# Attention with gated experts: the products with V of a pair in four groups instead of nine, and a batch's gating over more steps

## The chip, the cores and the metric

The kernel runs on one core of one Trainium2 chip. The metric is the device time of one execution in microseconds (us), the median over runs.

## The reference

Attention over 8 batches of 8 heads, 576 rows, head width 64, in which scores more than tau below their row's maximum are dropped; its output is the input of a mixture of 8 experts, of which each row takes the best two.

```python
scores = scale * np.matmul(q, k.transpose(0, 1, 3, 2))
thresh = np.max(scores, axis=-1, keepdims=True) - tau
scores = np.where(scores >= thresh, scores, -1000000000.0)
attn = np.exp(scores - np.max(scores, axis=-1, keepdims=True))
attn = attn / (np.sum(attn, axis=-1, keepdims=True) + 1e-09)
x = np.matmul(attn, v)                       # rows: 8 * 576, columns: 8 heads * 64
noisy = x @ w_gate + np.log1p(np.exp(x @ w_noise)) * noise
top2 = ...                                   # the two largest of 8, softmax over the two
out[mask] += weight * (np.maximum(x[mask] @ w1[e], 0.0) @ w2[e])     # per expert e
```

## The kernel before

Two heads of a batch are a **pair**; there are 32 pairs, four to a batch. The 2 x 576 score rows of a pair are cut into 9 tiles of 128 rows: tile j = 0 holds the last 64 rows of both heads, tiles 1 to 8 the first 512 rows of the two heads in turn. One tile is one **step**. Pair n begins at step g = 9n, and everything else that belongs to it is placed at a step counted from g, by the table `SCHED` and the loop at the end of `attention`. Steps of successive pairs overlap: what pair n does in its step 12 stands in step 3 of pair n + 1. Below, **place** p (0 to 8) is the step modulo 9, so the places of a pair's own tiles.

Within a step the phases run in the order (0, 1, 2, 3, 4, 5, 8, 6, 7), and each engine executes its own instructions in exactly that order:

- phase 0: `oev` (L387), ScalarE copies a finished half of the products with V out of PSUM into `ot`.
- phase 1: `scores` (L247), TensorE, one step ahead of the rest: tile j + 1 goes into one of two double banks `sp`. Each of two column halves takes two matmuls (L271), tile 0 three.
- phase 2: `rowmax`: VectorE scales the scores and takes the row maximum (L282), ScalarE takes exp (L284). Phase 3: `mask` (L307), VectorE, two steps behind. Phase 4: `threshold` (L292), ScalarE.
- phase 5: the products with V, the gating, the norm of the rows and `xlpart`/`xev`.
- phase 8: loads and `split_q`, `split_k`: ScalarE makes the high part of the next pair's q and k (L186, L198), GpSimd the low part, SyncE's queue spreads them (L220). k is at place 0 and q at place 2.
- phase 6: `ptile` (L310), three steps behind: TensorE transposes the masked tile in four parts (L319) into a PSUM bank and ScalarE copies it out (L322; L324 and L325 for tile 0). Phase 7: `pcorner` (L340 to L342) and `prem` (L333, L334), the same for the columns left over.

**The products with V.** `avpiece(n, i, kt)` (L385) multiplies one of five row blocks kt of V with one of two column pieces i of the transposed tiles (320 and 256 columns). Each call is a matmul for either head, in 64 of the array's columns each, and the hardware runs each as two: the profile shows four. The fifth block, `ptr`, uses 64 rows as well. `SCHED["av"]` gives the step of each call, `oev` the step of the copy. `xlpart` (L404, L405) then transposes the two halves of `ot` back and multiplies them with the gate's weights, at the steps `xl`; its first half has two blocks of 128, its second half two of 128 and one of 64.

**PSUM banks.** Four banks `tp0` to `tp3` serve all of these: `bank` takes the one that was released longest ago, when the program is written, and `done` gives it back. A product with V holds its bank from the first block to its `oev`; the others take and release theirs in one step.

**Gating.** At the end of a batch nine stages (L514 to L622) turn the gate's logits into slots; they go between GpSimd, VectorE, ScalarE and TensorE. Ten `gate_put` calls (L627, L628) on GpSimd's queue then write the table of slots. Before, stage i stands at step x + i + (i > 3), x being the step behind the second `xl`, and the first put at x + 11. The last two batches' puts and the last batch's stages have steps of their own (`START`, `LAST`), which the change leaves alone. The experts' first work is counted from step G = 288; their first read of the table, `tokens` (L837, SyncE's queue), stands at G - 35 = 253.

Of the kernel before, what the change touches and what calls it, by code (L numbers as in the profile page):

```python
# [43 lines left out]
WARM = 10  # L44

SCHED = dict(
    lag=2, mlag=2, lead=1, corner=8, rem=11, norm=11, av=((10, 11, 12, 13, 14), (15, 17, 17, 18, 19)), oev=(15, 20),
    xl=(16, 22), q=2, k=0, oevp=0, pieces=((0, 320), (320, 576)), order=(0, 1, 2, 3, 4, 5, 8, 6, 7),
    rec=12, xs=4, qsc="act", qs=0)


LAST = dict(
    av=((11, 11, 12, 12, 12), (12, 12, 12, 12, 12)), oev=(13, 13), xl=(14, 14), rec=13, norm=12)
# [7 lines left out]
    gate=(6, 7, 7, 8, 9, 9, 10, 11, 11), put=(12, 12, 12, 13, 13, 13, 13, 13, 13, 13), tokb=13, ixb=17,  # L61
# [4 lines left out]
@with_exitstack  # L66
def tile_attention_moe(ctx: ExitStack, tc, q, k, v, tau, wgn, noise, noise_r, w1, w2, out, x_dram, table, stage):
    nc = tc.nc
    const = ctx.enter_context(tc.tile_pool(name="const", bufs=1))
    cap = CAP  # L70
    nover = -(-max(N - cap, 0) // 128)
    slots = cap + 128 * nover
    state = dict(cap=cap, nover=nover, slots=slots)
    with tc.manual_schedule(), ExitStack() as c:
        work = c.enter_context(tc.tile_pool(name="work", bufs=1))
        psum = c.enter_context(tc.tile_pool(name="psum", bufs=1, space=PSUM))
        experts = Experts(tc, const, work, psum, state, w1, w2, out, x_dram, table, stage)
        attention(tc, const, work, psum, state, q, k, v, tau, wgn, noise, noise_r, out, x_dram, table, experts)
        experts.run(lambda: overflow_count(tc, const, work, state) if nover else None)
    if nover:  # L80
        with ExitStack() as c:
            overflow(c, tc, const, state, w1, w2, out, x_dram, table)
# [23 lines left out]
def early_batches():  # L106

    return max(B - 2, 0)
# [22 lines left out]
def attention(tc, const, work, psum, state, q, k, v, tau, wgn, noise, noise_r, out, x_dram, table, experts):  # L131
# [91 lines left out]
    xl = work.tile([128, HP, 32], F32, name="xl", tag="xl")  # L223
# [142 lines left out]
    ot, av = {}, {}  # L366
# [270 lines left out]
    def at(g, phase, f, *a):  # L637
        ev.setdefault((g, phase), []).append((f, a))
# [9 lines left out]
    lag = SCHED["lag"] + MLAG - 1  # L648
    G = 9 * NP
# [5 lines left out]
    for n in range(NP):  # L655
        g = 9 * n
        for j in range(9):
            at(g + j - d["lead"], 1, scores, n, j)
            at(g + j, 2, rowmax, n, j)
            at(g + j + MLAG, 3, mask, n, j)  # L660
            at(g + j, 4, threshold, n, j)
            at(g + j + lag, 6, ptile, n, j)
        at(g + d["corner"], 7, pcorner, n)
        at(g + d["rem"], 7, prem, n)
        at(g + d["norm"], 5, norm, n)
        at(g + d["rec"], 5, invert, n)
        if n == NP - 1:
            d = dict(SCHED, **LAST)
        for i in range(len(PIECES)):
            for kt in range(5):  # L670
                at(g + d["av"][i][kt], 5, avpiece, n, i, kt)
            at(g + d["oev"][i], d["oevp"], oev, n, i)
        for i in range(2):
            at(g + d["xl"][i], 5, xlpart, n, i)
            at(g + d["xl"][i], 5, xev, n, i)
        if n + 2 < NP:
            at(g if n else 9, 2, load, n + 2)
        if n + 1 < NP:
            at(g + d["qs"], 8, scale_q, n + 1)
            at(g + d["q"], 8, split_q, n + 1)  # L680
            at(g + d["q"], 8, spread, n + 1, "qs", [nc.sync])
            at(g + d["k"], 8, split_k, n + 1)
            at(g + d["k"], 8, spread, n + 1, "ks", [nc.sync])
        for f in parts[cut[n]:cut[n + 1]]:
            at(g + 6, 8, f)
        if n % HP == HP - 1:
            b = n // HP
            x = d["xl"][1] + 1
            for i in range(NB):
                at(g + x + (0 if b >= early_batches() else SCHED["xs"] + 2 * i), 5, xstore, b, i)  # L690
            late = experts and n == NP - 1
            if b == early_batches():
                at(g + x, 5, bump)
            for i, f in enumerate((gate_sum, gate_abs, gate_exp, gate_soft, gate_max, gate_hot, gate_rank,
                                   gate_slot, gate_slot2)):
                at(G + START["gate"][i] if late else g + x + i + (i > 3), 5, f, b)
            for i in range(2 * NB):
                to = g + x + 11 + i
                if experts and b >= B - 2:
                    to = G + START["put" if late else "put0"][i]  # L700
                at(to, 5, gate_put, b, i // 2, i % 2)
# [516 lines left out]
```

## Time and profile before

| | us |
|---|---|
| median of 3 runs | 1482.6 |
| lowest and highest run | 1479.03, 1483.6 |
| profiled execution | 1472.27 |
| its span, first to last instruction | 1470.5 |
| granted TensorE clock, mean | 0.993 |

The attention's 32 pairs take the first 606 us or so, the experts the rest; from about 525 us on the experts' first reads of the table, gathers and weights stand between the attention's instructions. The profile gives busy time by engine, an ordered list of instructions with their start (the timeline), and the waits. A bracket at the end of a timeline row is the idle time of that engine ahead of the instruction and what ended it; a row without one started without a wait. Matmuls overlap, so their durations add up to more than the time they take: what counts is from one start to the next. "128\*64" behind an operation is the part of the array used, rows by columns.

### The profile page before, as it was taken

What the parts mean: (1) busy time and instruction counts of PE and PEld (TensorE: products, weight loads), DVE (VectorE), ACT (ScalarE), POOL (GpSimd) and SP (SyncE); (2) the same over time, 40 slices, a digit from 0 to 9 for tenths busy, and PEclk for the clock granted to TensorE, in tenths of its full rate; (3) what the DMA queues carried; (4) which work ended last, traced back from release to release, by engine and by line L of the source; (5) the groups of instructions that cost most, each with busy time, mean ns of one, the idle gap of its engine ahead of it and who ended that gap; (6) DMA issues with size and microseconds to landing.
All of it is one profiled execution on the core that took longest, in us unless ns stands there. A gap on an engine that the chain in (4) does not pass through costs nothing. (4 is left out here: it accounts for less than half of the span.)

```text
span 1470.5 us, 26196 instructions
## 1 busy us (share of the span) xinstructions
PE 1435.7 (98%) x8750; PEld 1187.0 (81%) x8750; DVE 886.9 (60%) x2477; ACT 702.3 (48%) x1447; POOL 661.1 (45%) x1040
## 2 busy tenths in 40 slices
PE   8999999999999999997999999999999999999995
PEld 6777676767677776786998999999999989989884
DVE  7888888888888888644554344454454543543410
ACT  7888888888888887421222122132232221221210
POOL 4337575757575766454152262252342522521612
PEclk9999999999999999999999999999999999999998
DMA  7768686868686757356666376386375474573422
GB/s 198 188 164 214 164 223 161 218 168 223 161 217 165 193 154 194 83 123 149 172 150 152 86 164 147 87 186 157 81 186 142 115 171 120 133 170 89 69 29 31
DMA packets 189512, 220.48 MB, mean 150 GB/s; under 512 B 64453, under 2 KB 112541, under 8 KB 188353
## 3 DMA queue, kind: packets, MB, share of 16 engines
q1 hardware_dynamic: 162176, 178.91, 44.6%
q0 software_dynamic: 27200, 39.88, 16.3%
q8 instruction: 71, 1.16, 0.3%
q14 instruction: 65, 0.52, 0.1%
HBM read 103.25 MB, written 60.61 MB: 111 GB/s over the span
## 5 line engine op out<-in xcount | busy, mean ns | idle before, releaser
L284 ACT ACTIVATE e<-ns,nm 128x576 f32<-128x576 f32 x288 | 223.2, 775 | 37.1 <-DVE ns L282 34.4
L307 DVE SCALAR_TENSOR_TENSOR p<-ns,thr,e 128x576 f32<-128x576 f32 x256 | 222.3, 869 | 21.6 <-ACT thr L292 20.8
L282 DVE TENSOR_SCALAR_CACHE_REDUCE ns<-sp 128x576 f32<-128x576 f32 x288 | 214.4, 744 | 22.1 <-PE sp L271 17.7
L319 PEld LDWEIGHTS tp<-ident,p 128*128 128x128 f32 x1024 | 110.3, 143 | 99.7 <-ACT ot L391 23.1
L322 ACT ACTIVATE pt<-tp 128x512 f32<-128x512 f32 x256 | 150.9, 590 | 54.3 <-PE tp L319 53.5
L385 PE MATMUL tp<-pt,vt 128*64 128x256 f32 (+1 forms) x1024 | 176.5, 429 | 0.0
L319 PE MATMUL tp<-ident,p 128*128 128x128 f32 x1024 | 167.6, 286 | 0.0
L271 PE MATMUL sp<-ks,qh 128*128 128x288 f32 x496 | 159.6, 335 | 2.9 <-DVE ns L282 2.9
L963 POOL DMA_INDIRECT out<-m_y,ix x54 | 87.7, 1623 | 151.5 <-DVE m_y L1001 138.7
L963 POOL DMA_INDIRECT out<-m_y,sx x43 | 67.7, 1574 | 194.7 <-DVE m_y L944 160.3
L271 PE MATMUL sp<-ks,ql 128*128 128x288 f32 x496 | 138.3, 296 | 0.2 <-DMA ql<-loq 0.2
L923 ACT ACTIVATE m_p<-m_tp 128x384 fp32r<-128x384 f32 (+1 forms) x66 | 32.6, 494 | 211.1 <-PE m_tp L921 211.0
L944 DVE TENSOR_SCALAR m_y<-m_sp,gw 128x512 f32<-128x512 f32 (+1 forms) x43 | 32.3, 751 | 152.8 <-PE m_sp L942 144.2
L199 POOL TENSOR_TENSOR lok<-kr,hik 128x640 fp32r<-128x640 f32 x31 | 57.3, 1849 | 139.7 <-ACT hik L198 139.3
L871 POOL DMA_INDIRECT m_p<-x_rows,sx x71 | 70.1, 987 | 83.2 <-DMA stage<-m_p 45.5
L271 PEld LDWEIGHTS sp<-ks,qh 128*128 128x128 f32 x496 | 93.7, 189 | 5.0 <-DVE ns L282 3.2
L628 POOL DMA_INDIRECT slot_table<-pay,sl x80 | 87.8, 1097 | 17.5 <-issue 10.8
L271 PEld LDWEIGHTS sp<-ks,ql 128*128 128x128 f32 x496 | 94.2, 190 | 0.4 <-issue 0.4
L923 ACT ACTIVATE m_qh<-m_tp 128x384 fp32r<-128x384 f32 (+1 forms) x11 | 5.6, 506 | 181.8 <-PE m_tp L921 181.8
L385 PEld LDWEIGHTS tp<-pt,vt 128*64 128x64 f32 x1024 | 57.0, 136 | 42.6 <-issue 26.2
L921 PE MATMUL m_tp<-m_pt,m_pt 128*128 128x384 f32 (+1 forms) x396 | 72.6, 340 | 0.0
L921 PE MATMUL m_tp<-m_vt,m_pt 128*128 128x384 f32 (+1 forms) x264 | 71.7, 346 | 0.0
(386 smaller groups left out, 3503.2 us busy)
## 6 DMA issues: line engine op xcount, KB each, us to landing
m_qr<-w SPq DMA_DIRECT2D x85, 256.0 KB
qh<-hiq SPq DMA_DIRECT2D x124, 144.0 KB
ql<-loq SPq DMA_DIRECT2D x124, 144.0 KB
stage<-m_p SPq DMA_DIRECT2D x63, 256.0 KB
m_kr<-w SPq DMA_DIRECT2D x43, 256.0 KB
kr<-k SPq DMA_DIRECT2D x32, 320.0 KB
out<-zeros SPq DMA_DIRECT2D x19, 512.0 KB
qr<-q SPq DMA_DIRECT2D x32, 288.0 KB
```

The costliest lines, as they stand in the source:

```text
L199: nc.gpsimd.tensor_tensor(lo, x, hi.bitcast(F32), op=ALU.subtract)
L271: nc.tensor.matmul(o, q_, k_, start=(i == 0), stop=(i == len(parts) - 1))
L282: nc.vector.tensor_scalar(ns, sp[:, :, 0:HALF], -1.0 / math.sqrt(D), None, op0=ALU.mult, op1=ALU.min, accum_out=nm)
L284: nc.scalar.activation(e, ns, AF.Exp, bias=nm, scale=-1.0)
L307: nc.vector.scalar_tensor_tensor(p, ns, thr, e, op0=ALU.is_le, op1=ALU.mult, accum_out=ssum[n][:, c:c + 1])
L319: nc.tensor.transpose(tp[:, kt, :], p[:, 128 * kt:128 * kt + 128], ident)
L322: nc.scalar.activation(pt[n][:, s, :, c0:c0 + 128], tp, AF.Copy)
L385: nc.tensor.matmul(o[64 * s:64 * s + 64, 0:c1 - c0], w, x, start=(kt == 0), stop=(kt == 4))
L628: st = nc.gpsimd.indirect_dma_start(out=table, out_offset=bass.IndirectOffsetOnAxis(ap=d["sl"][0:m, i, c:c + 1], axis=0), in_=d["pay"][0:m ...
L871: self.nc.gpsimd.indirect_dma_start(out=r[0:m], out_offset=None, in_=x, in_offset=bass.IndirectOffsetOnAxis(ap=self.tok[e][2][0:m, t:t + 1 ...
L921: nc.tensor.matmul(ps[:, 0:n], w[:, 128 * c:128 * c + 128], x[:, c, 0:n], start=(i == 0), stop=(i == len(ops) - 1))
L963: st = self.nc.gpsimd.indirect_dma_start(out=out, out_offset=bass.IndirectOffsetOnAxis(ap=idx, axis=0), in_=y, in_offset=None, compute_op= ...
```

## The change

Two tables and the two lines that read them are edited. Products with V: piece 0 goes from steps 10, 11, 12, 13, 14 to 11, 11, 13, 13, 13, piece 1 from 15, 17, 17, 18, 19 to 15, 15, 17, 17, 17. The copies go from 15 and 20 to 14 and 18, the second `xl` from 22 to 21; the first stays at 16. By place, the products stood at 1 (two pairs' at once), 2, 3, 4, 5, 6, 8 and 0 and stand at 2, 4, 6 and 8 now; the copy of piece 1 goes from place 2 to place 0 and the second `xl` from place 4 to place 3. The gating's stages, counted from the pair's g, go from 23, 24, 25, 26, 28, 29, 30, 31, 32 to 22, 24, 25, 26, 28, 29, 32, 33, 35, the first of the ten puts from 34 to 37.

```diff
 SCHED = dict(
-    lag=2, mlag=2, lead=1, corner=8, rem=11, norm=11, av=((10, 11, 12, 13, 14), (15, 17, 17, 18, 19)), oev=(15, 20),
-    xl=(16, 22), q=2, k=0, oevp=0, pieces=((0, 320), (320, 576)), order=(0, 1, 2, 3, 4, 5, 8, 6, 7),
-    rec=12, xs=4, qsc="act", qs=0)
+    lag=2, mlag=2, lead=1, corner=8, rem=11, norm=11, av=((11, 11, 13, 13, 13), (15, 15, 17, 17, 17)), oev=(14, 18),
+    xl=(16, 21), q=2, k=0, oevp=0, pieces=((0, 320), (320, 576)), order=(0, 1, 2, 3, 4, 5, 8, 6, 7),
+    rec=12, gate=(0, 2, 3, 4, 6, 7, 10, 11, 13), put=15, xs=4, qsc="act", qs=0)
...
-                at(G + START["gate"][i] if late else g + x + i + (i > 3), 5, f, b)
+                at(G + START["gate"][i] if late else g + x + SCHED["gate"][i], 5, f, b)
             for i in range(2 * NB):
-                to = g + x + 11 + i
+                to = g + x + SCHED["put"] + i
```

TensorE, before, at places 2 to 4 of one pair. `tp2_3471` is bank tp2, its tile numbered 3471; `p` and `pr` are masked tiles (`pr` is tile 0), and the words in brackets name the engines whose semaphores the instruction waits on.

```order
L319 MATMUL tp1_3465<-ident_100,p_135 128x128 [waits DVE_49,Activation_49]
...
L333 MATMUL tp2_3471<-ident_100,p_135 128x128 [waits Activation_49]
...
L385 MATMUL tp0_3423<-pt1_3235,vt0_1687 64x320 x2
L319 MATMUL tp3_3500<-ident_100,pr0_3443 128x128 [waits DVE_49,Activation_49]
...
L404 MATMUL tp1_3518<-ident_100,ot0_3296 128x2x64 [waits Activation_49]
...
L385 MATMUL tp0_3423<-pt1_3235,vt0_1687 64x320 x2
L319 MATMUL tp2_3529<-ident_100,p_135 128x128 [waits DVE_49,Activation_49]
```

The same places of the same pair in the changed kernel:

```order
L319 MATMUL tp2_3465<-ident_100,p_135 128x128 [waits DVE_49,Activation_49]
...
L333 MATMUL tp3_3471<-ident_100,p_135 128x128 [waits Activation_49]
...
L404 MATMUL tp0_3489<-ident_100,ot0_3270 128x2x64 [waits Activation_49]
...
L319 MATMUL tp2_3507<-ident_100,pr0_3440 128x128 [waits DVE_49,Activation_49]
...
L385 MATMUL tp1_3444<-pt1_3236,vt0_1693 64x320 x4
L385 MATMUL tp1_3444<-ptr1_3237,vt0_1693 64x320 [waits Activation_49]
L385 MATMUL tp1_3444<-ptr1_3237,vt0_1693 64x320
L319 MATMUL tp3_3531<-ident_100,p_135 128x128 [waits DVE_49,Activation_49]
```

The products with V (L385) have left place 3, and `xlpart` (L404) has come into it, ahead of the transposes of tile 0. In the changed kernel those go into tp2, the bank of tile 8's transposes one place earlier. Before, they had tp3, and the next user of tile 8's bank was `xlpart` at place 4.

ScalarE, before, from exp of tile 0 at place 0 (the first row) to the copy of tile 8 at place 2 (the last but one):

```order
L284 ACTIVATE e0_3383<-ns0_3379,nm0_3380 128x576 [waits DVE_49,Activation_49]
L292 ACTIVATE thr0_3381<-nm0_3380,atau_120 128x1
L186 ACTIVATE qr1_3115<-qr1_3115,scale_118 128x576 [waits DMAHW0_49]
L198 ACTIVATE hik0_3395<-kr1_3114 128x640 [waits DMAHW2_49,DMAHW3_49,DMAHW1_49,Pool_49]
L322 ACTIVATE pt1_3235<-tp1_3403 128x4x128 [waits PE_49]
L284 ACTIVATE e1_3418<-ns1_3414,nm1_3415 128x576 [waits DVE_49,Activation_49]
L322 ACTIVATE pt1_3235<-tp2_3426 128x4x128 [waits PE_49]
L391 ACTIVATE ot0_3296<-tp3_3311 128x256
L284 ACTIVATE e2_3440<-ns2_3438,nm1_3415 128x576 [waits DVE_49,Activation_49]
...
L198 ACTIVATE hiq0_3449<-qr1_3115 128x576 [waits DMAHW1_49,DMAHW6_49,DMAHW0_49,DMAHW7_49,Activation_49,Pool_49]
L322 ACTIVATE pt1_3235<-tp1_3465 128x4x128 [waits PE_49]
L334 ACTIVATE ptr1_3236<-tp2_3471 128x512 [waits PE_49]
```

And the same stretch in the changed kernel:

```order
L391 ACTIVATE ot0_3270<-tp2_3305 128x256
L284 ACTIVATE e0_3384<-ns0_3380,nm0_3381 128x576 [waits DVE_49,Activation_49]
L292 ACTIVATE thr0_3382<-nm0_3381,atau_120 128x1
L186 ACTIVATE qr1_3116<-qr1_3116,scale_118 128x576 [waits DMAHW0_49]
L198 ACTIVATE hik0_3396<-kr1_3115 128x640 [waits DMAHW2_49,DMAHW3_49,DMAHW1_49,Pool_49]
L322 ACTIVATE pt1_3236<-tp3_3404 128x4x128 [waits PE_49]
L284 ACTIVATE e1_3419<-ns1_3415,nm1_3416 128x576 [waits DVE_49,Activation_49]
L322 ACTIVATE pt1_3236<-tp0_3424 128x4x128 [waits PE_49]
L284 ACTIVATE e2_3437<-ns2_3435,nm1_3416 128x576 [waits DVE_49,Activation_49]
...
L198 ACTIVATE hiq0_3449<-qr1_3116 128x576 [waits DMAHW1_49,DMAHW6_49,DMAHW0_49,DMAHW7_49,Activation_49,Pool_49]
L322 ACTIVATE pt1_3236<-tp2_3465 128x4x128 [waits PE_49]
L334 ACTIVATE ptr1_3237<-tp3_3471 128x512 [waits PE_49]
```

The copy of piece 1 (L391) has moved from between the copies of places 1 and 2 to the head of the stretch. What stands between tile 5's copy at place 8 and tile 8's copy at place 2 is the same set of instructions in both kernels (the two corner copies, L341 and L342, stand just ahead of both pieces).

## The prediction

> **What bounds the kernel now.** I read the page first, then the stages, TensorE's waits, and the timelines of TensorE and ScalarE over one pair.
>
> ```profile
> span 1470.5 us, 26196 instructions
> PE 1435.7 (98%) x8750; PEld 1187.0 (81%) x8750; DVE 886.9 (60%) x2477; ACT 702.3 (48%) x1447; POOL 661.1 (45%) x1040
> ```
>
> The shares are means over attention and experts, so they say little of a change in the attention. A stretch in its middle does (busy time of PE, PEld, DVE, ACT, POOL in 50 us):
>
> ```profile
> 300.00:350.00 50.00, 50.00 (x375) 35.28 (x374) 44.39 (x135) 43.55 (x93) 31.40 (x64) 1.00 0.75 198
> ```
>
> TensorE has no gap, VectorE is busy for 89%, ScalarE for 87%. Who is waited for shows in TensorE's waits from 40 to 560 us (total, times, longest):
>
> ```profile
> PE sp L271 <- DVE ns L282: 1.5, 4, 0.7
> ```
>
> In 520 us that is all that matters: TensorE's own instructions set the pace. One pair of them, its steps beginning with an L271:
>
> ```profile
> 303.01 0.66 PE L319 MATMUL tp<-ident,p 128*128 128x128 f32 x4
> 303.50 0.60 PE L333 MATMUL tp<-ident,p 128*128 128x128 f32 x4
> 303.86 0.38 PE L271 MATMUL sp<-ks,qh 128*128 128x288 f32 x1
> ...
> 304.56 0.76 PE L385 MATMUL tp<-pt,vt 128*64 128x320 f32 x4
> 305.25 0.66 PE L319 MATMUL tp<-ident,pr 128*128 128x128 f32 x4
> 305.67 0.38 PE L271 MATMUL sp<-ks,qh 128*128 128x288 f32 x1
> ...
> 311.73 0.38 PE L271 MATMUL sp<-ks,qh 128*128 128x288 f32 x1
> ...
> 312.21 0.29 PE L271 MATMUL sp<-ks,ql 128*128 128x288 f32 x1
> 312.34 0.27 PE L404 MATMUL tp<-ident,ot 128*128 128x128 f32 x1
> ...
> 312.88 0.64 PE L319 MATMUL tp<-ident,p 128*128 128x128 f32 x4
> 313.27 0.38 PE L271 MATMUL sp<-hik,qd 128*128 128x288 f32 x1
> ...
> 314.24 1.08 PE L385 MATMUL tp<-pt,vt 128*64 128x256 f32 x8
> 315.26 0.66 PE L319 MATMUL tp<-ident,p 128*128 128x128 f32 x4
> 315.75 0.27 PE L340 MATMUL tp<-ident,pr 128*64 128x128 f32 x1
> 315.78 0.38 PE L271 MATMUL sp<-ks,qh 128*128 128x288 f32 x1
> ...
> 321.75 0.60 PE L333 MATMUL tp<-ident,p 128*128 128x128 f32 x4
> ...
> 324.52 0.27 PE L404 MATMUL tp<-ident,ot 128*128 128x128 f32 x1
> ```
>
> From L333 to L333 a pair takes 18.25 us (303.50 to 321.75). Scores take 0.61 (311.73 to 312.34), the transposes of a tile 0.39 (312.88 to 313.27): 1.00 for a step with nothing else. The tail of the attention already shows products with V packed closely, and a second half of xlpart alone:
>
> ```profile
> 606.29 1.30 PE L385 MATMUL tp<-pt,vt 128*64 128x320 f32 x8
> 607.52 0.76 PE L385 MATMUL tp<-ptr,vt 64*64 64x320 f32 x4
> 608.21 1.95 PE L385 MATMUL tp<-pt,vt 128*64 128x256 f32 x16
> 610.08 0.65 PE L385 MATMUL tp<-ptr,vt 64*64 64x256 f32 x4
> 610.66 0.45 PE L921 MATMUL m_sp<-m_vt,m_ql 128*128 128x384 f32 x1
> ...
> 614.97 0.27 PE L404 MATMUL tp<-ident,ot 128*128 128x128 f32 x1
> ...
> 615.94 0.44 PE L921 MATMUL m_sp<-m_vt,m_hik 128*128 128x384 f32 x1
> ```
>
> **Fewer groups on TensorE.** Eight rows of 256 columns take 1.02 (314.24 to 315.26), four take 0.58 (610.08 to 610.66). Four more rows cost 0.44, so 0.14 of the 0.58 is the group's own. Going in costs 0.09 (303.86 to 304.56 is 0.70, against 0.61), the transposes behind it 0.03 more (305.25 to 305.67). A group costs 0.26. A call of 320 columns is 0.69 - 0.14 = 0.55, and changing to ptr's 64 rows within a group 1.23 - 2 x 0.55 = 0.13.
>
> Before, a pair has eight such excursions: places 1, 2, 3, 4, 5, 6, 8 and 0, that at place 4 shared with xlpart's block of 64. After, it has the four groups, and that block stands alone: five. Changes of rows within a group go from one to two. TensorE saves 3 x 0.26 - 0.13 = 0.65 a pair, to 17.60.
>
> The Trainium skill (TensorEngine Tiling (Array Packing), Key Properties) says that changing the tiling mode, not just the tile, drains TensorE. For the products with V the trace agrees (0.26 a group). It does not for every instruction in 64 columns: L340 begins 0.49 after four transposes that otherwise take 0.39, and the scores start 0.03 later. By this rule alone fewer groups pay: that is the first rival.
>
> **The new wait.** The order shows that tile 0's transposes at place 3 now go into the bank of tile 8's at place 2, so they wait for ScalarE's copy of tile 8. Its queue ahead of that copy:
>
> ```profile
> 315.95 0.60 ACT L322 ACTIVATE pt<-tp 128x512 f32<-128x512 f32 x1 [0.58 <-PE tp L319]
> ...
> 320.68 0.38 ACT L391 ACTIVATE ot<-tp 128x256 f32<-128x256 f32 x1
> ...
> 322.37 0.59 ACT L322 ACTIVATE pt<-tp 128x512 f32<-128x512 f32 x1
> ...
> 326.76 0.60 ACT L322 ACTIVATE pt<-tp 128x512 f32<-128x512 f32 x1 [1.06 <-PE tp L319]
> ```
>
> The first row is tile 5's copy at place 8, released by transposes that began at 315.26. From there to tile 8's copy (322.37, the fifteenth) none of the rows has a wait: corner copies, exp, the high parts of q and k, two more copies, L391. The copy ends at 322.96, 7.70 after the transposes of place 8 began. The change moves L391 within this stretch and takes nothing out, so 7.70 stays.
>
> Before, the next to take that bank was xlpart at 324.52, 1.56 behind the copy's end: no wait. After, TensorE gets from the transposes of place 8 to those of tile 0 sooner:
>
> - corner and step change 0.52 (315.26 to 315.78), places 0 and 1 1.00 each;
> - place 2: 0.70, eight rows of 320 columns 1.23, transposes and L333 0.85 (303.01 to 303.86): 2.78;
> - place 3: scores 0.61, xlpart with its block of 64 0.97 (614.97 to 615.94).
>
> That is 6.88; the bank comes at 7.70. How fast TensorE starts behind a release shows only in VectorE's case, an accumulator read and the matmul that it let go:
>
> ```profile
> 589.87 0.08 DVE L282 DVE_READ_ACCUMULATOR ns<-sp 128x1 f32 x1
> ```
> ```profile
> 590.00 0.40 PE L271 MATMUL sp<-ks,qh 128*128 128x288 f32 x1 [0.38 <-DVE ns L282]
> ```
>
> I take 0.05 (589.95 to 590.00), bounds 0 and three times that, 0.15. TensorE waits 0.87 a pair, more than the 0.65 saved. From tile 0's transposes it goes on undisturbed to place 8's, which start ScalarE's queue anew:
>
> - the transposes 0.42;
> - place 4: 0.70, eight rows and four of ptr 1.92 (606.29 to 608.21), transposes 0.42: 3.04;
> - place 5: 1.00; place 6: 0.70 + 1.02 + 0.42 = 2.14; place 7: 1.54 (311.73 to 313.27);
> - place 8: 0.97 to the products (313.27 to 314.24), 1.02 for eight rows, 0.58 for ptr: 2.57.
>
> Together 10.71. This ring, 10.71 on TensorE, 7.70 on ScalarE, 0.05 to hand over, is the new period: 18.46, 0.21 above 18.25. With the bounds, and 0.1 for what adjacent rows may be misread by, it is 0.06 to 0.41 above.
>
> The Trainium skill (TensorEngine Tiling (Array Packing), PSUM Bottleneck) says that tiling speeds up TensorE but not PSUM evacuation. Before, the trace shows no wait of that kind; the ring is what the rule would be here.
>
> **The other waits.** L333 and xlpart now follow copies that stand ahead of tile 8's in the same queue: what they wait comes out of the 0.87, not on top of it. With two short steps in a row, the scores of place 2 come soon behind the row maximum of tile 1 that frees their bank (mean of one, in ns, behind the bar):
>
> ```profile
> L282 DVE TENSOR_SCALAR_CACHE_REDUCE ns<-sp 128x576 f32<-128x576 f32 x288 | 214.4, 744 | 22.1 <-PE sp L271 17.7
> ```
>
> Tile 1's scores end 0.77 after place 0 begins (311.73 to 312.50), the maximum 0.74 later, and TensorE is there after 2.00: 0.4 to spare.
>
> **The gating.** Its instructions stay; their spacing changes.
>
> ```profile
> 28.09 0.60 PE L333 MATMUL tp<-ident,p 128*128 128x128 f32 x4
> ...
> 560.80 0.60 PE L333 MATMUL tp<-ident,p 128*128 128x128 f32 x4
> ```
> ```profile
> DVE p L307 <- ACT thr L292: 18.2, 30, 1.2
> ...
> DVE xr L418 <- POOL spacer L627: 9.8, 5, 2.7
> ```
>
> 29 pairs take 532.7, 18.37 each: 3.5 more in all than 29 x 18.25. Part is the rank's matmuls, which stay; part is VectorE at xev behind GpSimd's puts (the last row, the only large wait that the gating makes). The puts keep their number and one still stands just ahead of the copies that xev needs, but place 8 is now 3.1 long and covers a late VectorE. Bounds: a gain of 3.5 and none; I take 1.0. The last put of batch 5 moves to step 253, where SyncE's queue reads the table:
>
> ```profile
> slot_table<-pay,sl POOLq DMA_INDIRECT x80, 4.3
> ```
>
> A put lands 4.3 after its issue, so that read, and the spread of pair 29's q behind it, may come 3 to 4 later; q is needed at step 261, seven steps or 14 us on. I cost it at nothing; without that cover it would be 4, once.
>
> **The sum.** 29 x 0.21 = 6.1, less 1.0 for the gating. In the last two pairs the experts' work already makes TensorE wait, with bounds of 2 either way; I take 0. So 5.1 more: 1472.3 to 1477.4 for the profiled execution. The median is 10.3 above that execution, and I add the same 5.1 to it: 1487.7.
>
> **Rivals.**
>
> *The bank wait doesn't bind* (0.12): ScalarE's stretch ends by 6.88, or TensorE gets its bank otherwise. Then 31 pairs x 0.65 = 20 and the gating's 1.0 are gained: 1461.6. For it: TensorE is the bound before, and the groups' cost is plain in the rows. Against it: the stretch has no idle time to lose and would have to be 0.87 shorter. It decides from there: at 0.21 shorter the period is 18.25.
>
> *The two parts cancel* (0.22): the ring is at its low end (29 x 0.06 = 1.7) and the gating gives back 2 to 3: 1482. For it: gating pairs run over 18.25 today. Against: only VectorE's lateness shows there, and the ring is a sum of rows.
>
> *The wait is passed on* (0.06): exp and thr behind the held copies come late and VectorE's masks wait for them, as they already do (18.2 in 30 waits, 0.6 each). If half of one reaches TensorE in every pair, 0.3 more, it is 29 x 0.51 = 15 and 1497. Against: ScalarE catches up from place 4 on, where it waited 1.06 at 326.76.
>
> **How the numbers follow.** The forecast has 0.60. A measurement tells about 0.3%, 4.4, from no change; 5.1 is just beyond it, so of the 0.60 I give 0.10 to no change. Slower: 0.50 + 0.06 = 0.56; same: 0.10 + 0.22 = 0.32; faster: 0.12. The range: low, 29 x 0.06 - 3.5 - 2 = -3.8, 1479; high, 29 x 0.41 + 2 = 13.9, 1496. It leaves out the first rival and the last.
>
> **What would show it.** TensorE's waits: tile 0's transposes (L319, pr) at ScalarE's copies (L322), about 0.87 each, 29 times or so; 18.46 from L333 to L333; a group of eight rows at 1.02 and 1.23; L322 at place 2 ending 7.70 after place 8's transposes begin. If that wait is missing and the period near 17.6, I am wrong; if it is there but under 0.6, the sizes are.

## The result, and the profile after

| us | before | after |
|---|---|---|
| median of 4 runs | 1483.09 | 1494.84 |
| lowest and highest run | 1479.03, 1483.6 | 1494.08, 1496.8 |
| profiled execution | 1472.27 | 1495.13 |
| granted TensorE clock, mean | 0.993 | 0.989 |

The ratio after to before is 1.0101, with a 95% interval from 1.0082 to 1.0120: the change costs 15 (12 to 18), where the prediction had 5.1. The two traces differ by 22.9, since the profiled execution of before was faster than all its timed runs; sizes below are taken from ratios and from the traces of several kernels. The clock isn't the cause: the kernel before, profiled once more (e0 below), took 1479.95 at a mean of 0.988.

The page after, and 50 us in the middle of the attention (busy time of PE, PEld, DVE, ACT, POOL):

```profile
span 1493.4 us, 26202 instructions
PE 1426.1 (95%) x8750; PEld 1201.7 (80%) x8750; DVE 877.8 (59%) x2477; ACT 700.7 (47%) x1447; POOL 667.3 (45%) x1040
```
```profile
300.00:350.00 50.00, 46.58 (x347) 34.30 (x346) 39.41 (x119) 40.31 (x86) 30.92 (x57) 1.00 0.61 168
```

TensorE, without a gap in these 50 us before, now has 3.4 us of gaps. Whom it waits for, from 40 to 575 us (total, times, longest):

```profile
PE tp L319 <- ACT pt L322: 24.0, 27, 1.4
```

That is the forecast wait of tile 0's transposes at the copy of tile 8: 0.80 in plain pairs (0.87 forecast), 1.04 to 1.41 in six others, which make the mean 0.89. One pair without puts on TensorE, from the transposes of place 8 and L333 to the next of each:

```profile
265.74 0.66 PE L319 MATMUL tp<-ident,p 128*128 128x128 f32 x4
...
270.63 0.60 PE L333 MATMUL tp<-ident,p 128*128 128x128 f32 x4
...
273.50 0.66 PE L319 MATMUL tp<-ident,pr 128*128 128x128 f32 x4 [0.80 <-ACT pt L322]
...
284.35 0.66 PE L319 MATMUL tp<-ident,p 128*128 128x128 f32 x4
...
289.24 0.49 PE L333 MATMUL tp<-ident,p 128*128 128x128 f32 x3
```

and on ScalarE, tile 5's copy and tile 8's:

```profile
266.43 0.60 ACT L322 ACTIVATE pt<-tp 128x512 f32<-128x512 f32 x1 [0.83 <-PE tp L319]
...
272.86 0.58 ACT L322 ACTIVATE pt<-tp 128x512 f32<-128x512 f32 x1
```

Tile 8's copy ends at 273.44, 7.70 after the transposes at 265.74, the figure of the forecast to the hundredth, and TensorE goes on 0.06 later. This pair holds the matmuls of the gating's rank stage and takes 18.61 (270.63 to 289.24); plain ones, without them, take 18.40 (18.25 before). So the ring is there: 29 x 0.15, some 4 of the 15.

The rest lies in two pairs of each batch. In the first, GpSimd's copies of the row norms stand behind a put:

```profile
297.00 1.09 POOL L628 DMA_INDIRECT slot_table<-pay,sl  x1 [0.16 <-POOL spacer L627]
...
298.49 0.19 POOL L361 COPY rn<-ssum 64x4 f32<-64x4 f32 x1
302.36 0.18 POOL L362 COPY rn<-ssum 64x4 f32<-64x4 f32 x1 [3.69 <-DMA slot_table<-pay,sl]
```

The copy that reads the upper 64 rows (L362) waits 3.69 until the put ahead of it has landed, that is, until its transfer has ended. VectorE's `xev` needs the copies (its row names the spacer L627, the next instruction on GpSimd) and stands in front of the row maximum, from which ScalarE takes exp; behind that exp waits tile 5's copy, the start of the stretch:

```profile
302.70 0.49 DVE L418 TENSOR_TENSOR xr<-tp,rn 128x320 f32<-128x320 f32 x1 [3.09 <-POOL spacer L627]
```
```profile
303.96 0.78 ACT L284 ACTIVATE e<-ns,nm 128x576 f32<-128x576 f32 x1 [2.89 <-DVE xr L418]
304.65 0.28 ACT L292 ACTIVATE thr<-nm,atau 128x2 f32<-128x2 f32 x1
304.83 0.58 ACT L322 ACTIVATE pt<-tp 128x512 f32<-128x512 f32 x1
```

TensorE is held at two points:

```profile
302.75 0.66 PE L319 MATMUL tp<-ident,p 128*128 128x128 f32 x4
...
309.21 0.60 PE L333 MATMUL tp<-ident,p 128*128 128x128 f32 x4
...
312.61 0.66 PE L319 MATMUL tp<-ident,pr 128*128 128x128 f32 x4 [1.39 <-ACT pt L322]
...
328.45 0.60 PE L333 MATMUL tp<-ident,p 128*128 128x128 f32 x4
```

From the transposes of place 8 to L333 it takes 6.46 in place of the plain pair's 4.89 (265.74 to 270.63), 1.57 more, and this pair takes 19.97 (289.24 to 309.21). VectorE's rows, where it has read out a row maximum, and TensorE's scores of places 0, 1 and 2:

```profile
303.78 0.08 DVE L282 DVE_READ_ACCUMULATOR ns<-sp 128x1 f32 x1
...
305.20 0.08 DVE L282 DVE_READ_ACCUMULATOR ns<-sp 128x1 f32 x1
...
306.62 0.08 DVE L282 DVE_READ_ACCUMULATOR ns<-sp 128x1 f32 x1
```
```profile
303.92 0.40 PE L271 MATMUL sp<-ks,qh 128*128 128x288 f32 x1 [0.37 <-issue]
...
305.34 0.41 PE L271 MATMUL sp<-ks,qh 128*128 128x288 f32 x1
...
306.76 0.40 PE L271 MATMUL sp<-ks,qh 128*128 128x288 f32 x1
```

VectorE works without a gap from 302.70 on, 1.42 a step (row maximum and mask), and the scores start 0.06 behind each of its reads. Place 0 starts 0.64 late, and places 0 and 1 take 1.42 each in place of 0.97.

In the next pair (19.24) tile 0 waits 1.39 in place of 0.80. ScalarE had ended the instruction ahead of tile 8's copy by 311.34, and the transposes had begun at 308.71, but the copy starts 0.61 later, and its row names only an `xlpart` matmul:

```profile
310.66 0.68 ACT L198 ACTIVATE hiq<-qr 128x576 fp32r<-128x576 f32 x1
311.95 0.60 ACT L322 ACTIVATE pt<-tp 128x512 f32<-128x512 f32 x1 [0.61 <-PE tp L405]
```

It is so in all six batches (2.8 in six). Last, six puts in a row (302.95 to 310.9 on GpSimd) make the following norm late; the other 0.25 of this pair falls behind that:

```profile
314.48 0.21 DVE L357 RECIPROCAL ssum<-ssum 128x9 f32<-128x9 f32 x1 [1.59 <-POOL ssum L352]
```

From 40 to 560 us, VectorE's wait at `xev` and GpSimd's at the put, after:

```profile
DVE xr L418 <- POOL spacer L627: 17.3, 6, 3.2
```
```profile
POOL rn L362 <- DMA slot_table<-pay,sl: 20.7, 6, 3.8
```

The prediction showed 9.8 for the first of these before. The second, before:

```profile
POOL rn L362 <- DMA slot_table<-pay,sl: 16.4, 6, 3.6
```

So the wait itself isn't new. The four pairs of each of the first five batches in this stretch, L333 to L333, take 75.9 to 76.4 in the trace, against 73.1 to 74.3 before.

### The profile page after: what moved, and what is told of

Its sections match the earlier page's. It is cut to its first block, busy times and chain, and to the rows that moved or that the text cites. A ratio compares the mean times of both kernels' runs of the same rounds, so it can differ in the third digit from the quotient of the medians.

```text
span 1493.4 us, 26202 instructions
## 1 busy us (share of the span) xinstructions
PE 1426.1 (95%) x8750; PEld 1201.7 (80%) x8750; DVE 877.8 (59%) x2477; ACT 700.7 (47%) x1447; POOL 667.3 (45%) x1040
## 5 line engine op out<-in xcount | busy, mean ns | idle before, releaser
L307 DVE SCALAR_TENSOR_TENSOR p<-ns,thr,e 128x576 f32<-128x576 f32 x256 | 218.3, 853 | 34.6 <-ACT thr L292 28.5
L319 PEld LDWEIGHTS tp<-ident,p 128*128 128x128 f32 x1024 | 114.9, 143 | 61.3 <-issue 32.0
L319 PE MATMUL tp<-ident,p 128*128 128x128 f32 x1024 | 162.7, 281 | 1.0 <-DVE p L307 0.6
L385 PE MATMUL tp<-pt,vt 128*64 128x256 f32 (+1 forms) x1024 | 153.2, 420 | 0.0
L199 POOL TENSOR_TENSOR lok<-kr,hik 128x640 fp32r<-128x640 f32 x31 | 52.3, 1687 | 137.9 <-ACT hik L198 137.5
L385 PEld LDWEIGHTS tp<-pt,vt 128*64 128x64 f32 x1024 | 62.8, 136 | 46.5 <-issue 19.9
L628 POOL DMA_INDIRECT slot_table<-pay,sl x80 | 83.3, 1042 | 16.7 <-issue 12.6
```

The lines of the kernel that those rows point to most:

```text
L199: nc.gpsimd.tensor_tensor(lo, x, hi.bitcast(F32), op=ALU.subtract)
L307: nc.vector.scalar_tensor_tensor(p, ns, thr, e, op0=ALU.is_le, op1=ALU.mult, accum_out=ssum[n][:, c:c + 1])
L319: nc.tensor.transpose(tp[:, kt, :], p[:, 128 * kt:128 * kt + 128], ident)
L385: nc.tensor.matmul(o[64 * s:64 * s + 64, 0:c1 - c0], w, x, start=(kt == 0), stop=(kt == 4))
L628: st = nc.gpsimd.indirect_dma_start(out=table, out_offset=bass.IndirectOffsetOnAxis(ap=d["sl"][0:m, i, c:c + 1], axis=0), in_=d["pay"][0:m ...
```

## The experiments

Every kernel was timed against the kernel before on the same chip. "29 pairs" is L333 to L333 in the trace, from pair 1 to pair 30; the step of the first put is counted from a pair's start. The kernel before itself took from 1474.99 to 1483.09 beside them ("before", median), so kernels are compared by the ratio, not by their us.

| run | products with V | first put | L362, L363 | us | before | ratio, 95% interval | 29 pairs |
|---|---|---|---|---|---|---|---|
| before again | old | 34 | GpSimd | 1479.88 | 1480.80 | 0.9997 (0.9978, 1.0015) | 536.5 |
| the change | new | 37 | GpSimd | 1494.84 | 1483.09 | 1.0101 (1.0082, 1.0120) | 547.8 |
| e1 | new | 34 | GpSimd | 1497.51 | 1480.80 | 1.0119 (1.0096, 1.0143) | 546.4 |
| e2 | old | 37 | GpSimd | 1494.07 | 1480.80 | 1.0084 (1.0061, 1.0108) | 551.0 |
| e4 | new, q later | 37 | GpSimd | 1496.93 | 1480.80 | 1.0105 (1.0084, 1.0126) | 550.2 |
| e5 | new | 37 | VectorE | 1481.18 | 1475.91 | 1.0035 (1.0021, 1.0049) | 537.6 |
| e6 | old | 34 | VectorE | 1474.77 | 1475.91 | 0.9987 (0.9972, 1.0002) | 532.4 |
| e7 | old | 37 | VectorE | 1477.88 | 1475.91 | 1.0011 (0.9996, 1.0025) | 536.1 |
| e8 | new, q later | 37 | VectorE | 1474.57 | 1475.91 | 0.9994 (0.9980, 1.0009) | 532.6 |
| e9 | new, other bank | 37 | VectorE | 1511.99 | 1481.60 | 1.0219 (1.0194, 1.0243) | 560.8 |
| e10 | old | 37, heap | VectorE | 1481.76 | 1481.60 | 0.9997 (0.9982, 1.0013) | 534.3 |
| e11 | old | 37, stages old | GpSimd | 1492.73 | 1481.60 | 1.0069 (1.0047, 1.0091) | 550.5 |
| e12 | new, other bank | 37 | VectorE | 1483.16 | 1474.99 | 1.0053 (1.0040, 1.0066) | 536.8 |
| e13 | new, other bank | 37 | GpSimd | 1494.29 | 1474.99 | 1.0119 (1.0100, 1.0138) | 550.9 |
| e14 | new, other bank, q later | 37 | VectorE | 1478.07 | 1475.54 | 1.0017 (1.0006, 1.0029) | 536.0 |
| e15 | as e14, stages later | 37 | VectorE | 1475.87 | 1475.54 | 1.0005 (0.9990, 1.0021) | 529.4 |

**The parts apart.** The first theory was that the ring makes the time; its rival, that the puts three steps later do.

> The kernel before, unchanged, as a yardstick: the profiled execution of before took 1472, its timed runs 1479 to 1484, while the profiled execution of the change agrees with its timed runs. Both theories expect 1483 within 3. If its profile is again near 1472, a profile of this kernel is faster than its timed runs and the two traces can't be subtracted; if it is near 1483, the trace shows where the 10 us sit (a stretch with a lower granted clock, or single waits).

The kernel before, run again as it was, is where it was. In its trace the pairs of the puts take 18.25 to 22.03: the late `xev` is there too (14.5 in six waits), and what TensorE pays for it is unsteady.

e1 has the new products with V and the gating at its old steps:

```diff
-    rec=12, gate=(0, 2, 3, 4, 6, 7, 10, 11, 13), put=15, xs=4, qsc="act", qs=0)
+    rec=12, gate=(1, 2, 3, 4, 6, 7, 8, 9, 10), put=12, xs=4, qsc="act", qs=0)
```

> The products with V, their copies and the second xlpart as changed; the gating and the puts at the steps of before. Ring theory (the wait of tile 0's transposes for ScalarE's copy of tile 8 closes a ring of 18.4 us, which has no slack, so that every lateness of VectorE behind GpSimd's puts lengthens a pair): 18.40 in pairs without puts, about 0.9 at each of these waits, the pair with the puts 1 to 1.5 over that, the pair behind it not, so 1487 to 1491. Puts theory (the new spacing of gating and puts makes nearly all of the loss, the ring just the 0.15 a pair): 1485 to 1488 with no pair over 18.8.

e2 has the old products with V and the gating and puts at their new steps:

```diff
-    rec=12, xs=4, qsc="act", qs=0)
+    rec=12, gate=(-1, 1, 2, 3, 5, 6, 9, 10, 12), put=14, xs=4, qsc="act", qs=0)
```

> The gating's stages and the puts as changed; the products with V, their copies and the second xlpart at the steps of before. Ring theory: the old order has 1.5 us of slack between the copy of tile 8 and the next use of its bank, which takes up the lateness; 18.25 in pairs without puts, less than 0.6 over it with them; 1482 to 1486. Puts theory: the pair with the puts and the one behind it are 1 to 1.7 and 0.8 longer here too, 6 times: 1490 to 1497.

Each part alone costs as much as both, so they don't add. e1 is slower than either theory had it. It has the ring (plain pairs 18.40) and the late `xev` (14.3 in six waits; the pairs of the puts take 18.5 to 19.7), and the rank, which stands at place 3 there, makes a wait of its own, from 40 to 575 us:

```profile
PE tp L319 <- ACT pt L322: 15.8, 21, 0.8
PE tp L585 <- POOL mb L578: 7.0, 6, 1.2
```

The new steps take the rank to place 5 and this wait away. That isn't the gain that the prediction put at 1.0, which was for VectorE's wait at `xev`; in time, the change is 0.18% below e1, no more than the two intervals leave open. But e2, without any ring (plain pairs 18.25), is 0.84% slower than before all the same, as the puts theory had it. The ring theory falls as an account of the whole.

e4 tests the ring's size. q's split leaves the stretch:

```diff
-    xl=(16, 21), q=2, k=0, oevp=0,
+    xl=(16, 21), q=3, k=0, oevp=0,
```

> The changed kernel with the split of q one step later (place 3), which takes one instruction of 0.57 us on ScalarE out of the stretch ahead of tile 8's copy and leaves TensorE's work as it is. Ring theory: the wait of tile 0's transposes falls from 0.9 to 0.3, the period from 18.40 to 17.83, about 16 us less than the change over 29 pairs if the pairs with puts gain as well: 1478 to 1484. Puts theory: the pairs with puts stay at 19.9 and 19.25, so at most half of it: 1487 to 1492. If the ring is not what sets the period: no change, 1495.

Two plain pairs early on show what was expected: one takes 17.84, as a ring of 7.70 less one split of 0.57 has it, one 17.47, with no wait of TensorE. From there on pairs take 18.0 to 20.6 and nothing is gained, so both theories' times are missed; what holds these pairs, e4 doesn't tell.

**The wait for the landing.** The second theory names L362. It and L363 go to VectorE in e5 (the changed kernel), e6 (before) and e7 (e2):

```diff
-        eng.tensor_copy(x[0:64, 1, 1:5], r[64:128, 4:8])
-        eng.tensor_copy(x[0:64, 1, 0:1], r[64:128, 8:9])
+        nc.vector.tensor_copy(x[0:64, 1, 1:5], r[64:128, 4:8])
+        nc.vector.tensor_copy(x[0:64, 1, 0:1], r[64:128, 8:9])
```

> The changed kernel with one edit: the two copies of the row norms that read the upper 64 rows (L362 and L363) go from GpSimd to VectorE; L362 is the one that waits for a put to land. Landing theory (the extra time of the changed kernel over the 18.4 of its plain pairs comes from that wait: xev late, then the puts in a heap, then lok and norm late): VectorE's wait at xev (L418 behind L627) is gone, the pair of the puts goes from 20.0 to 18.6 and the next from 19.25 to 18.6 or less, six batches x 2.1 = 12.6 are gained and the time is 1480 to 1486; the ring's own wait (L319 behind L322, 0.9 a pair) stays. Spacing theory (the stages and puts cost by themselves where they now stand, with or without that wait): 1492 to 1496.

> The kernel before with the same edit (L362 and L363 on VectorE). Landing theory: it loses its own late xev (14.5 us of VectorE's waits in six, of which the pairs show 0 to 4 each), every pair of the puts is 18.25, and the time falls to 1474 to 1479. Spacing theory: no late xev matters there, 1479 to 1484.

> The kernel before with the new spacing of the gating and puts alone (products with V as before) and the same edit (L362 and L363 on VectorE). Landing theory: the 13 us that this spacing costs by itself are the wait for the landing and the heap of puts behind it; they go, 1475 to 1483. Spacing theory: 1490 to 1495.

In all three VectorE's wait at L418 behind L627 is gone, and every pair, with puts or without, takes 4.89 (e5) or 6.49 (e6, e7) from place 8 to L333. In e5 the ring's wait stays as it was (40 to 575 us) and is nowhere over 0.81; its pair of the puts takes 18.85 and ends at the first of the two L333, the next takes 18.40:

```profile
PE tp L319 <- ACT pt L322: 23.3, 29, 0.8
```
```profile
305.32 0.60 PE L333 MATMUL tp<-ident,p 128*128 128x128 f32 x4
...
323.72 0.49 PE L333 MATMUL tp<-ident,p 128*128 128x128 f32 x3
```

The times of the landing theory came out in each run, but they were written for a kernel before of about 1480 us, and here it took 1475.91; by ratio, too, the spacing theory falls in e5 and e7, while e6 can't tell the two apart. With the puts at 37 this wait costs 0.66% (the change against e5, where 12.6 us, 0.85%, had been expected), 0.73% (e2 against e7) and 0.66% (e13 against e12): some 10 us, whatever the products with V. With the puts at 34 and the old products it costs 0.13% (before against e6, an interval that just holds zero); with the puts at 34 and the new products (e1) no run takes it out.

**Puts or stages, and the heap.** e11 moves only the puts against the kernel before (first put 37, stages where they were; first cut). e10 is e7, without a wait for a landing, but with six puts at one step, the heap that this wait makes (second cut):

```diff
-    rec=12, xs=4, qsc="act", qs=0)
+    rec=12, gate=(0, 1, 2, 3, 5, 6, 7, 8, 9), put=14, xs=4, qsc="act", qs=0)
```
```diff
-put=14, xs=4, qsc="act", qs=0)
+put=(14, 15, 16, 20, 20, 20, 20, 20, 20, 23), xs=4, qsc="act", qs=0)
```

> The kernel before with one edit: the first put three steps later (37 in place of 34), the stages where they were. If the cost of the new spacing lies in the puts (three ahead of the copies of the row norms in place of six, so six behind them in one heap): 1486 to 1496, as with the whole new spacing. If it lies in the stages (the rank at place 5, the stages that GpSimd runs between): 1476 to 1484, as before.

> The kernel before with the new spacing of the gating, L362 and L363 on VectorE (no wait for a landing), and six of the ten puts at one step: at 37, 38, 39, six at 43 and the last at 46, which is the heap that the wait for the landing made by itself. Heap theory (six puts in a row are what costs: lok, the norm and with them VectorE come late, and ScalarE's copy at place 1 is released late while they run): the pair of the puts at 19.5 or more, six batches x 1.2 or more, 1484 to 1492. Landing theory (only the late xev costs; a heap behind it lies beside other work): 1475 to 1481, as with single puts.

The puts do it, not the stages. The heap alone costs nothing (e10; it stands some 4 us earlier against TensorE's places than in e11), and a late `xev` with four puts behind it next to nothing (0.13%); the two together cost 0.7% (e2, e11).

**Another bank.** `xl` (16, 23) gives tile 8's bank to tile 1's transposes at place 4, and tile 0's take tile 7's. e9 does so with the stages moved along (gate 0, 2, 3, 4, 6, 7, 9, 10, 11), e12 with the stages nearly where they were, e13 as e12 without the two copies' edit (the cut shows e12 and e13):

```diff
-    xl=(16, 21), q=2, k=0, oevp=0,
+    xl=(16, 23), q=2, k=0, oevp=0,
-    rec=12, gate=(0, 2, 3, 4, 6, 7, 10, 11, 13), put=15, xs=4, qsc="act", qs=0)
+    rec=12, gate=(-1, 1, 1, 2, 4, 5, 8, 9, 11), put=13, xs=4, qsc="act", qs=0)
```

> The changed kernel with the second xlpart two places later (place 5, steps 16 and 23), so that the bank of tile 8's transposes goes to tile 1's at place 4 and tile 0's at place 3 take tile 7's; L362 and L363 on VectorE; the gating's stages at 24, 26, 27, 28, 30, 31, 33, 34, 35, the puts from 37 as in the changed kernel. Ring theory (the four groups save 0.65 to 0.75 a pair on TensorE, and only the bank at place 3 takes it back): no wait of L319 (pr) for L322, plain pairs 17.5 to 17.7, so 29 x 0.6 less than 18.25, 1455 to 1465. Rival (another engine sets 18.0 or more as soon as TensorE gets faster: VectorE is busy for 16.2 of a pair, ScalarE for 16): 1470 to 1478.

> The other bank again (second xlpart at place 5, steps 16 and 23; L362 and L363 on VectorE), but the gating's stages nearly where the changed kernel has them (23, 25, 25, 26, 28, 29, 32, 33, 35, puts from 37), so that GpSimd's part of the soft stage stands at place 8 again and not behind the low part of k at place 1. Ring theory with the gating's mishap of the run before mended: plain pairs at 17.86 as there, pairs of a batch within 0.6 of that, VectorE's wait for L545 gone; 29 x 0.4 less than with the two copies alone: 1458 to 1468. If the gating costs the same with any table once TensorE is faster: 1478 or more.

> As e12_bank_gates_kept, but with L362 and L363 back on GpSimd, so that VectorE's xev is late again behind the landing of a put, now without the ring at place 3. If the lateness costs through the ring (ScalarE's stretch starts late and the bank comes late): within 2 us of e12. If it reaches TensorE directly, by masks that come late in the short steps at places 0 and 1, or by late copies: the pair of the puts 1 to 2 longer, 6 to 12 us more than e12.

In all three the wait for tile 8's copy is gone; plain pairs take 17.85 in e9 and e12, 17.57 in e13. e9 missed by its gate table: VectorE waits for GpSimd's soft stage (40 to 560 us).

```profile
DVE gr L548 <- POOL gu L545: 21.9, 6, 3.7
```

e12 mends that. Three of a batch's four pairs take 18.2 to 19.4, so it missed too; VectorE waits for ScalarE's thresholds, as it did in e5 (39.1), and now TensorE for VectorE as well (0.4 in e5):

```profile
DVE p L307 <- ACT thr L292: 36.6, 21, 1.8
```
```profile
PE sp L271 <- DVE ns L282: 14.3, 20, 1.6
```

e13 is 0.66% slower than e12, within the 6 to 12 us expected, with the late `xev` back and no ring at place 3: the lateness reaches TensorE without the ring.

```profile
DVE xr L418 <- POOL spacer L627: 14.7, 6, 3.2
```

e14 moves q's split to place 3 as well, e15 also the middle stages a step (gate -1, 1, 2, 3, 5, 6, 8, 9, 11).

> As e12_bank_gates_kept, with q's split at place 3 in place of 2. If ScalarE's stretch costs in the batch's pairs (thr late at place 3): the waits of L307 for L292 at 1.75 shrink, these pairs go to 18.0 to 18.5, 1462 to 1472. If the gating's own work on VectorE costs: they stay at 19.0 or more, 1480 to 1486.

> As e14_bank_q3, with exp, soft, max and hot one step later each (26, 27, 29, 30) and the rank at 32, as in e8_q3_copies. If the wait is ScalarE's: the same as e14 within 3 us. If the steps of these stages decide: apart from e14 by more than that, either way.

Plain pairs of e14, L333 to L333, take 17.54:

```profile
83.54 0.60 PE L333 MATMUL tp<-ident,p 128*128 128x128 f32 x4
...
101.08 0.38 PE L333 MATMUL tp<-ident,p 128*128 128x128 f32 x2
```

The other pairs of a batch stay at 18.6 to 19.0 and eat most of it: e14 lies between its two expectations. VectorE's wait for the thresholds is shorter each time (1.29 against 1.74 in e12), not in sum:

```profile
DVE p L307 <- ACT thr L292: 38.6, 30, 1.8
```

e15 is 2.2 below e14, within the 3 expected; the pair with the rank falls from 19.0 to 18.3. e8 (e4 with the two copies on VectorE and five of the stages later) has 18.0 to 18.6 in the pairs of its batches. Its time is 0.6 over the 1474 expected, but the gain behind that number, 29 x 0.5, isn't there: the kernel before took 1475.91 beside it, and the 0.06% by which e8 is below it can't be told from none:

> The changed kernel with q's split and spread a place later (place 3, so that ScalarE's stretch is shorter), the gating's middle stages one step later (gate 0, 3, 4, 5, 7, 8, 10, 11, 13, so that VectorE doesn't wait for GpSimd's sums at place 6) and L362 and L363 on VectorE. Landing theory with the ring: plain pairs at 17.5 to 17.9 as with q later alone, no late pair beyond 18.5, so 29 x 0.5 less than before: 1462 to 1474. Spacing theory: the batches keep their late pairs, 1488 to 1496.

No version is measurably faster than the kernel before.

## Why the prediction was right in direction and short in size

- **TensorE's saving: right.** 0.65 a pair to 17.60 was forecast; where nothing holds TensorE, pairs take 17.47 to 17.54 (e4, e14).
- **The new wait and the ring: right.** 7.70 on ScalarE, 0.87 of wait, 18.46 were forecast; 7.70, 0.80 and 18.40 came. 29 x 0.21 = 6.1 was a little high: TensorE's share of the ring is 10.65 (255.09 to 265.74), not 10.71, so a plain pair costs 0.15, and e5 against e7, the new products with V without the late copies, is 0.24%, 3.5. The rule cited there from the Trainium skill (TensorEngine Tiling (Array Packing), PSUM Bottleneck), that tiling doesn't speed up PSUM evacuation, agrees with it: the copy out of the bank ends 7.70 on in both kernels.
- **The gating: wrong, and this is the mis-sized term.** "Less 1.0 for the gating", with bounds of a gain of 3.5 and none. It cost some 11 (3.5 + 9.8 - 1.9): the spacing 0.24% (3.5, e7 against e6), and the wait for the landing 0.66% (9.8, the change against e5) where it cost 0.13% (1.9) before. With the ring's 3.5 these make 14.9; that they meet the 15 proves nothing, since the four ratios are links of one chain from before to the change, each known to about 0.2%, 3 us. The order of the links matters, too: taken behind the new products, the gating's new steps cost nothing that can be told (the change against e1): in e1 the late VectorE slows TensorE already, and the rank's wait comes on top.
- **The step that failed** is "place 8 is now 3.1 long and covers a late VectorE". The late VectorE was seen, and the put just ahead of the copies too, but nothing covers it: without its wait the changed kernel is 9.8 faster (e5). Before, the same stretch already took 6.85 to 7.60 in place of 6.49 in four batches. The traces show what the change adds. With the old products and a late `xev` (before, e2, e11), place 0 starts late, by up to 1.1 before and 1.9 in e11, and places 0 and 1 then keep their length (1.72 and 2.38; plain 1.70 and 2.38). With the new ones (the change, e1, e13) place 0 starts late as well, and the two places, which have lost their products, then go at VectorE's pace, up to 1.42 each in place of 0.97. "0.4 to spare" for these short steps counts VectorE's row maximum alone; with the mask it needs 1.42 a step, and has nothing to catch up with. e13 loses 1.9 to 2.6 from place 8 to L333 in five of six batches, without the ring at place 3. e2 and e11 lose a further 1.0 to 2.6 at place 2, by another road (below).
- **The bounds of the gating** had no loss in them: the order had the put ahead of the copies in both kernels, but how many puts come behind the wait changed from four to seven.
- **The rivals.** The bank wait binds; the parts don't cancel; "the wait is passed on" (1497) came nearest in time, but by another mechanism: plain pairs lose 0.15, not its 0.51.
- **Luck.** Without the wait for the landing the change costs 0.35%, 5.2, nearly the 5.1 forecast; but that is 3.5 for the ring and 3.5 for the spacing, less the 1.9 that before pays for its own late `xev`, where the forecast had 6.1 less 1.0. And 1494.84 is still below the range's upper end, 1496, only because that end allows the ring 0.41 a pair.

What stays open: in e2 and e11 place 2 takes 2.9 to 4.5 in place of 1.89, because ScalarE's copy of tile 7 starts 1.1 to 2.7 after it could. In e11 its transposes run from 459.50, and ScalarE had ended its exp by 461.05:

```profile
462.95 0.60 ACT L322 ACTIVATE pt<-tp 128x512 f32<-128x512 f32 x1 [1.90 <-PE tp L319]
```

e10 has as many puts in a row and no such wait. No row names what holds the copy, and no run here tells it; the 0.61 of tile 8's copy in the change may be the same. Nor is it settled why the spacing costs 3.5 by itself (half of it lies in the last two of the 29 pairs of e7), what holds the pairs of e4, and what VectorE's wait for the thresholds costs in the batches of e12 to e15.

## What to carry to other kernels

A ring through two engines can be added up from rows beforehand: find who uses a bank next, and add both engines' shares. An instruction that waits for a transfer just ahead of it in its own queue is a debt that every later table can call in: price it for the new place, with a loss as one of the bounds, or take the wait out. When two steps lose work, add up what each of the other engines needs for a step: one that was quick enough for the long steps may set the pace of the short ones as soon as it is late.

## What the runs showed of the hardware that was not expected

- A put holds a copy behind it on GpSimd for 2.7 us each time before (16.4 in six) and 3.4 in the change (20.7 in six), though neither uses the other's data as far as the kernel's text shows. Two small copies on VectorE remove it (e5, e6, e7). The kernel before may also scatter less without it: 1472.49 to 1476.7 in 12 runs (e6), 1470.73 to 1482.82 in 35 of before beside them.
- ScalarE's late copies in e2, e11 and the change, above.
